# Late attention chunks with the state and the scores stacked on partitions, one product per head

## The chip, the cores and the metric

The kernel runs on one core of one Trainium2 chip. The time is device microseconds (us) of one execution; the figure for a kernel is the median of several runs. In the profile the engines are PE (TensorE matmul), PEld (TensorE weight load), DVE (VectorE), ACT (ScalarE), POOL (GpSimd) and SP (SyncE, which here issues DMAs). SBUF has 128 partitions; PSUM has eight banks of 512 float32 per partition.

## The reference

A linear attention with a decaying state, followed by an MLP with a cosine gate. B = 4 sequences, H = 8 heads, S = 768 steps, D = 48 per head; 3072 tokens of width 384, hidden width 2048.

```python
state = zeros(B, H, D, D)
for t in range(S):
    cur = u * k[t] (outer) v[t]
    y[t] = r[t] @ (state + cur)
    state = w * state + k[t] (outer) v[t]
h = y @ w_in
out = (h * cos(h)) @ w_out
```

`w` and `u` are per head and per element of D. The kernel computes the recurrence in chunks of steps: inside a chunk it needs the masked score matrix A (r times k, each with its share of the decay, above the diagonal; on the diagonal the sum over D of r, u and k, called the bonus here), y = A v + r state, and a new state = w^n (state + k v).

## The kernel before

The MLP takes most of the time. Weights are split in a high and a low part in a float32 format that TensorE runs in one pass, so each product is three matmuls: `mm_h` (L351, 9 matmuls of 384 columns for a block of three 128-token chunks and one 128-wide slice f of the hidden width) and `mm_o` (L357, 9 matmuls). One such step (n, f) has 18 of these. There are 8 blocks of 3 chunks and 16 slices; between `mm_h` and `mm_o` the gate runs over ACT and DVE (L362, L365, L368, L1273, L1276, L1279). Blocks 0 to 3 run interleaved while the weights arrive; blocks 4 to 7 run one after the other.

Attention chunks 0 to 11 (`chunk`) cover the first half of each sequence: one sequence, 128 steps, all 8 heads. Their outputs stay in 12 slots (`R_x`). Chunks 12 to 23 (`late_chunk`) come when slots are free: each covers two sequences (b = 0, 1) of 64 steps and all 8 heads. Before the change the two sequences share the partitions: partitions 0 to 63 hold the 64 steps of b = 0, 64 to 127 those of b = 1 (`half[b]`). Heads go in pairs p = 0 to 3 with parity j = 0, 1; a transposed operand has head j of a pair on partitions 64 j to 64 j + 47, for both sequences.

A late chunk before the change, with its lines:

- loads on SP's queue: pieces of k and r for the transposes (L974), and k, r, v with steps on partitions (L966), all after the score matmuls of the chunk before;
- DVE transposes k and r (L1010); POOL multiplies both with the decay (L1017);
- POOL: r k (L1029), k with its decay (L1035), times u (L1032); DVE sums to the bonus a (L1044);
- ACT writes the diagonals, one instruction per pair and parity: a times an identity (L1053);
- PE: 16 score matmuls, 48 rows high and 64 columns wide, on the four quarters of its array (L1070), and 16 for k v (L1083; the last two chunks leave these out, as no state is wanted after them);
- DVE copies the scores into A where step order allows (L1102, two instructions); ACT spreads the state into a zero-padded tile, parity by parity (L1112); DVE makes the new state (L1120, L1121);
- PE: the product, `mm_xx`: 24 matmuls of the spread state with r, both parities on 112 rows (L1132), then 32 of v with A, 64 rows, one sequence at a time (L1154), summed in the same PSUM banks. An output is written in strips of 32 of the 384 features; a strip that belongs to both heads of a pair gets one matmul from each;
- ACT and DVE write the result to the slots in the split format (L1171, L1176).

The order on each engine's queue is fixed when the kernel is built. `Plan` holds each piece of work as an `op` with engine, due time, modelled cost, what it waits for and its buffers. `one_pass` schedules greedily by earliest start and then by due time, `latest` turns a schedule into new due times (the latest start that keeps its end), and `order` makes FULL such passes, keeps the one with the earliest end, and then searches at random over the work that starts before HORIZON = 110 us. `port=True` marks work on DVE and POOL that the model keeps from overlapping. A `Buf` takes one tile of a ring, and the plan picks which.

Of the kernel before, what the change touches and what calls it, by code (L numbers as in the profile page):

```python
# [33 lines left out]
XS = 12  # L34
# [6 lines left out]
FULL = 6  # L41
HORIZON = 110.0
PASSES = 250
# [37 lines left out]
class Plan:  # L81
# [101 lines left out]
    def order(self, passes):  # L183
# [100 lines left out]
def kernel(  # L284
# [86 lines left out]
    with ExitStack() as actx:  # L371
# [20 lines left out]
        R_A = ring("A", 4, [P, NP, C], F32)  # L392
# [13 lines left out]
        zt = att.tile([KP, 2, NP, 2 * D], F32, name="zt")  # L406
        R_zt = [Tile(zt[:, n]) for n in range(2)]
        R_zt2 = [Tile(zt, R_zt)]
# [128 lines left out]

        def late_table():
            b_tab2 = Buf(B_ATT)

            def tab_t2():
                pt = b_tab2().rearrange("q (p t) -> q p t", p=NP)
                for p in range(NP):
                    for b in range(2):
                        nc.tensor.matmul(pt[b * CT : (b + 1) * CT, p, :], decT_k[:, p, mid], ident, start=True, stop=True)

            def tab_copy2():
                pt = b_tab2().rearrange("q (p j d) -> q (p j) d", p=NP, j=2)
                nc.scalar.copy(dec_k, pt[:, :, 0:D])
# [3 lines left out]
            return o_c2, op(POOL, 110, 0.6, start_late, [last_A[0]], port=True)  # L553
# [179 lines left out]
        def chunk(i, due, xbuf):  # L733
# [128 lines left out]
            def mm_x():  # L862
                x = xv()
                for g in range(NK * 4):
# [3 lines left out]
                        x[gs, g // 4, :], zb()[:, p, G * s : G * s + G], rT()[0:KP, p, :], start=(g < 4), stop=False,  # L868
# [80 lines left out]
        def late_chunk(i, due, xbuf):  # L949
            if not o_dk2:  # L950
                o_dk2.extend(late_table())
            o_late = o_dk2[1]
            m, n_ = (i - XS) % NM, (i - XS) // NM
            t0 = EC * C + n_ * CT
            kb, vb, mb, ab, rb = Buf(R_k), Buf(R_v), Buf(R_f), Buf(R_a), Buf(R_f)
# [4 lines left out]
            half = [slice(b * CT, (b + 1) * CT) for b in range(2)]  # L960
            more = i < NJ - NM

            def load(dst, src):
                def go():
                    for b in range(2):
                        nc.sync.dma_start(  # L966
                            dst()[half[b], :, 0:D], src[2 * m + b, :, t0 : t0 + CT, :].rearrange("h t d -> t h d")
                        )

                return go  # L970
# [31 lines left out]
            l_k = op(SP, due - 5.2, 1.3, load(kb, k), ahead, [kb], lat=2.6, line="late")  # L1002
            l_r = op(SP, due - 5.1, 1.3, load(rn, r), ahead, [rb], lat=2.6, line="late")
            l_v = op(SP, due - 5.0, 1.3, load(vb, v), ahead, [vb], lat=2.6, line="late")
# [9 lines left out]
            def decay_s(dst, dec):  # L1014
                def go():
                    d = late_t(dst)[0:KP]
                    nc.gpsimd.tensor_tensor(  # L1017
                        d, d, dec[0:KP, None, :, mid].to_broadcast([KP, 2, NP, CT]), op=ALU.mult
                    )

                return go

            t_k = op(DVE, due - 2.9, 1.1, tr_s(kT, ks), [l_ks], [ks, kT])
            e_k = op(POOL, due - 2.8, 1.4, decay_s(kT, decT_k), [t_k, o_dtk], [kT], port=True)
            t_r = op(DVE, due - 2.8, 1.1, tr_s(rT, rs), [l_rs], [rs, rT])
            e_r = op(POOL, due - 2.7, 1.4, decay_s(rT, decT_r), [t_r, o_dtr], [rT], port=True)
# [4 lines left out]
            def bonus_u():  # L1031
                nc.gpsimd.tensor_tensor(heads(mb), heads(mb), u_b, op=ALU.mult)  # L1032

            def decay_k():
# [4 lines left out]
            o_mu = op(POOL, due - 2.2, 1.05, bonus_u, [o_m, o_u], [mb], port=True)  # L1039
# [3 lines left out]
                0.5,  # L1043
# [5 lines left out]
            def diagonal(j):  # L1049
                def go():  # L1050
                    for p in range(NP):
                        h = 2 * p + j
                        nc.scalar.activation(A[j]()[:, p, 0:CT], ident2, AF.Copy, scale=ab()[:, h : h + 1])  # L1053
# [3 lines left out]
            o_d = [op(ACT, due - 1.55 + 0.01 * j, 1.1, diagonal(j), [o_a, o_late], [ab, A[j]], line="diagonal") for j in range(2)]  # L1057

            def score(j):
                return sp()[:, j, 0 : NP * CT].rearrange("q (p t) -> q p t", p=NP)  # L1060

            def z_of():
                return sp()[:, :, NP * CT : NP * (CT + D)].rearrange("q b (p e) -> q b p e", p=NP)

            def mm_az():
                for p in range(NP):
                    for j in range(2):
                        ps = slice(j * DP, j * DP + D)
                        for b in range(2):
                            nc.tensor.matmul(  # L1070
                                score(j)[half[b], p, :],
                                late_t(kT)[ps, b, p, :],
                                late_t(rT)[ps, b, p, :],
                                start=True,
                                stop=True,
                            )
                if not more:
                    return
                z = z_of()
                for p in range(NP):  # L1080
                    for j in range(2):
                        for b in range(2):
                            nc.tensor.matmul(  # L1083
                                z[j * DP : j * DP + DP, b, p, :],
                                kb()[half[b], 2 * p + j, :],
                                vb()[half[b], 2 * p + j, 0:D],
                                start=True,
                                stop=True,
                            )
# [4 lines left out]
                1.3 if more else 0.75,  # L1094
                mm_az,
                [e_k, e_r] + ([o_kd, l_v] if more else []),
                [kT, rT, sp] + ([kb, vb] if more else []),
# [3 lines left out]
            def mask(j):  # L1101
                return lambda: nc.vector.copy_predicated(  # L1102
                    A[j]()[:, :, 0:CT], upper2[:, None, :].to_broadcast([P, NP, CT]), score(j)
                )
# [3 lines left out]
            before = [last_z[2 * m], last_z[2 * m + 1], last_z2.get(m)]  # L1108

            def spread(j):  # L1110
                ps = slice(j * DP, j * DP + D)
                return lambda: nc.scalar.copy(zb()[ps, :, :, j * D : (j + 1) * D], zc[m][ps])  # L1112

            o_zt = [op(ACT, due - 1.9, 0.5, spread(j), before, [zb]) for j in range(2)]

            if more:

                def state():
                    w_c = pq[0:KP, None, :, 16:17].to_broadcast([KP, 2, NP, D])
                    nc.vector.tensor_tensor(zc[m], z_of()[0:KP], zc[m], op=ALU.add)  # L1120
                    nc.vector.tensor_tensor(zc[m], zc[m], w_c, op=ALU.mult)  # L1121

                last_z2[m] = op(DVE, due - 1.2, 1.2, state, [o_A, *o_zt, *before, o_pow], [sp])

            def mm_xx():
                x = xp()[:, :, 0 : NK * CT].rearrange("q b (kk t) -> q b kk t", kk=NK)
                for kk in range(NK):
                    for b in range(2):
                        for g in range(4 * kk, 4 * kk + 4):
                            p, s = divmod(g, 3)  # L1130
                            gs = slice(G * (g % 4), G * (g % 4) + G)
                            nc.tensor.matmul(  # L1132
                                x[gs, b, kk, :],
                                zb()[:, b, p, G * s : G * s + G],
                                late_t(rT)[0:KP, b, p, :],
                                start=(kk == 0),
                                stop=False,
                                skip_group_check=True,
                            )

# [6 lines left out]
                for group in rounds:  # L1147
                    for b in range(2):
                        for g, n in group:
                            p, s = divmod(g, 3)  # L1150
                            gs = slice(G * (g % 4), G * (g % 4) + G)
                            parts = {0: ((0, 0),), 1: ((0, G), (1, D)), 2: ((1, DP + 16),)}[s]
                            j, at = parts[n]
                            nc.tensor.matmul(  # L1154
                                x[gs, b, g // 4, :],
                                vb().rearrange("q h d -> q (h d)")[half[b], p * 2 * DP + at : p * 2 * DP + at + G],
                                A[j]()[half[b], p, 0:CT],
                                start=False,
# [4 lines left out]
            xo = op(PE, due - 0.7, 1.8, mm_xx, [e_r, l_v, *e_A, *o_zt], [rT, xp, vb, zb, *A], lat=0.3)  # L1163

            def xv():
                return xp()[:, :, 0 : NK * CT].rearrange("q b (kk t) -> q kk b t", kk=NK)
# [4 lines left out]
            x_h = op(ACT, due - 0.4, 0.47, lambda: nc.scalar.copy(xo_(0), xv()), [xo], [xp, xbuf])  # L1171
# [327 lines left out]
```

## Time and profile before

| | |
|---|---|
| median of 3 runs | 510.2 us (509.86 to 510.3) |
| the profiled execution | 509.76 us |
| its span, first to last instruction | 508.0 us |
| PE busy | 496.5 us, 98% of the span |
| DVE, ACT, POOL busy | 368.1, 328.4, 173.4 us |
| mean granted TensorE clock | 0.998 |

The span is shorter than the profiled execution by what lies before the first and after the last instruction. In a row of the profile, L351 is a line of the kernel, `out<-in` are tile names without buffer numbers, then partitions x elements. The words behind `<-` at the end name what ended the idle time before these instructions. Matmuls are pipelined, so their lengths overlap: the time that one takes from PE is the distance of the starts.

### The profile page before, as it was taken

To read this page: it belongs to the slowest core of one execution; us is meant where nothing else is said; L and a number is where in the kernel's file an instruction comes from. 1 tells how busy PE (TensorE), PEld (TensorE's weight loads), DVE (VectorE), ACT (ScalarE), POOL (GpSimd) and SP (SyncE) were. 2 spreads that over 40 slices of the span, in tenths; PEclk is the share of its full clock that TensorE was granted. 3 is DMA by queue.
4 is the path that set the end of the run, shared out by engine and by line. 5 is a ranking of instruction groups with operands and counts; after the bars stand their busy time and mean duration, and the time that the engine had idled before them with its cause. 6 is when DMAs were issued, how large, how long until landed. Compare 5 with 4: busy or idle time off the path is not lost.

```text
span 508.0 us, 14010 instructions
## 1 busy us (share of the span) xinstructions
PE 496.5 (98%) x5459; PEld 475.6 (94%) x5459; DVE 368.1 (72%) x775; ACT 328.4 (65%) x835; POOL 173.4 (34%) x186
## 2 busy tenths in 40 slices
PE   7999999999999999999999999999999999999994
PEld 5788889999999999999999999999999999999994
DVE  5898988889888865566676776776767757666552
ACT  3989887777767665546576565675756666654452
POOL 6785722365454342233425134223134042200000
PEclk9999999999999999999999999999999999999999
DMA  8987545587765583243576746546455563410001
GB/s 139 160 167 183 91 142 172 186 163 159 176 134 131 112 150 48 34 103 48 137 141 148 143 130 144 116 140 147 119 140 131 143 160 80 116 25 24 2 1 50
DMA packets 128041, 60.15 MB, mean 118 GB/s; under 512 B 103777, under 2 KB 123874, under 8 KB 127970
## 3 DMA queue, kind: packets, MB, share of 16 engines
q1 hardware_dynamic: 122694, 52.02, 42.5%
q0 software_dynamic: 5184, 7.08, 10.2%
q8 instruction: 44, 0.72, 0.6%
q14 instruction: 27, 0.22, 0.1%
q10 hardware_dynamic: 92, 0.10, 0.1%
HBM read 47.39 MB, written 11.80 MB: 116 GB/s over the span
## 4 chain that ended last, share of the span: by engine, by line
PE 95%; DVE 1%; DMA 1%; POOL 1%; ACT 0%; issue 0%; POOLq 0%; DVEq 0%
PE bank L357 41%; PE bank L351 39%; PE bank L880 2%; PE bank L846 2%; PE bank L1132 2%; PE bank L1154 2%; PE bank L772 2%; PE bank L1070 1%; PE bank L867 1%; DMA k<-in_k_dram 1%; PE bank L1083 1%; PE bank L902 1%; PE bank L1345 1%; POOL f L791 0%; POOL k L799 0%; DVE rT L781 0%
## 5 line engine op out<-in xcount | busy, mean ns | idle before, releaser
L357 PE MATMUL bank<-w_out_hi,gh 128*128 128x384 f32 x384 | 132.2, 344 | 0.0
L357 PE MATMUL bank<-w_out_hi,gl 128*128 128x384 f32 x384 | 129.8, 338 | 0.0
L351 PE MATMUL bank<-xh,w_in_lo 128*128 128x384 f32 x384 | 129.6, 337 | 0.0
L357 PE MATMUL bank<-w_out_lo,gh 128*128 128x384 f32 x384 | 129.4, 337 | 0.0
L351 PE MATMUL bank<-xh,w_in_hi 128*128 128x384 f32 x384 | 129.1, 336 | 0.0
L351 PE MATMUL bank<-xl,w_in_hi 128*128 128x384 f32 x384 | 128.7, 335 | 0.0
L362 ACT ACTIVATE qi<-bank 128x384 int32<-128x384 f32 (+1 forms) x132 | 63.2, 482 | 60.2 <-PE bank L351 60.1
L1273 DVE TENSOR_TENSOR bank<-bank,f 128x384 f32<-128x384 f32 (+1 forms) x132 | 72.8, 551 | 39.0 <-ACT f L368 36.1
L368 ACT ACTIVATE f<-f 128x384 f32<-128x384 f32 (+1 forms) x132 | 67.6, 515 | 43.1 <-DVE f L365 39.2
L365 DVE SCALAR_TENSOR_TENSOR f<-bank,qi 128x384 f32<-128x384 f32 (+1 forms) x132 | 71.1, 541 | 33.1 <-ACT qi L362 32.5
L1279 DVE TENSOR_TENSOR gl<-bank,gh 128x384 fp32r<-128x384 f32 (+1 forms) x132 | 71.1, 540 | 25.9 <-ACT gh L1276 25.5
L1276 ACT CAST gh<-bank 128x384 fp32r<-128x384 f32 (+1 forms) x132 | 61.6, 467 | 36.8 <-DVE bank L1273 35.1
L357 PEld LDWEIGHTS bank<-w_out_hi,gh 128*128 128x128 f32 x384 | 72.0, 187 | 2.5 <-DVE bank L1273 0.2
L351 PEld LDWEIGHTS bank<-xh,w_in_hi 128*128 128x128 f32 x384 | 72.1, 188 | 0.6 <-DVE A L853 0.2
L357 PEld LDWEIGHTS bank<-w_out_hi,gl 128*128 128x128 f32 x384 | 72.1, 188 | 0.3 <-DVE gl L1279 0.2
L351 PEld LDWEIGHTS bank<-xh,w_in_lo 128*128 128x128 f32 x384 | 72.2, 188 | 0.0
L351 PEld LDWEIGHTS bank<-xl,w_in_hi 128*128 128x128 f32 x384 | 72.1, 188 | 0.0
L357 PEld LDWEIGHTS bank<-w_out_lo,gh 128*128 128x128 f32 x384 | 72.0, 187 | 0.0
L695 POOL TENSOR_TENSOR f<-f,raw 128x384 int32<-128x384 int32 x32 | 36.3, 1135 | 62.3 <-DVE f L684 14.2
L1017 POOL TENSOR_TENSOR kT<-kT,decT_k 112x512 f32<-112x512 f32 x12 | 15.9, 1327 | 117.2 <-PE bank L351 63.5
L1329 POOL DMA_DIRECT2D out_dram<-f x36 | 32.0, 996 | 44.6 <-ACT f L1313 30.1
L836 ACT ACTIVATE A<-ident,a 128x128 f32<-128x128 f32 x96 | 29.4, 391 | 1.6 <-DVE a L827 1.5
(113 smaller groups left out, 596.3 us busy)
## 6 DMA issues: line engine op xcount, KB each, us to landing
raw<-in_moe_w_in_dram SPq DMA_DIRECT2D x32, 384.0 KB, 3.5
raw<-in_moe_w_out_dram SPq DMA_DIRECT2D x32, 384.0 KB, 3.4
out_dram<-f POOLq DMA_DIRECT2D x36, 192.0 KB, 4.4
raw<-in_k_dram SPq DMA_DIRECT2D x47, 80.0 KB, 2.6
raw<-in_r_dram SPq DMA_DIRECT2D x47, 80.0 KB, 3.3
k<-in_k_dram SPq DMA_DIRECT2D x12, 192.0 KB, 4.0
r<-in_r_dram SPq DMA_DIRECT2D x12, 192.0 KB, 4.2
v<-in_v_dram SPq DMA_DIRECT2D x12, 192.0 KB, 5.0
```

The costliest lines, as they stand in the source:

```text
L351: nc.tensor.matmul(ph, a, b_, start=(i == 0), stop=(i == len(mm) - 1))
L357: nc.tensor.matmul(acc, a[:, ts], b_[:, f, :], start=(first and i == 0), stop=(last and i == 2))
L362: nc.scalar.activation(qi, ph, AF.Copy, scale=INV_2PI, bias=0.25)
L365: nc.vector.scalar_tensor_tensor(q, ph, INV_2PI, qi, op0=ALU.mult, op1=ALU.subtract)
L368: nc.scalar.activation(q, q, AF.Sin, scale=TWO_PI, bias=0.5 * math.pi)
L695: lambda: nc.gpsimd.tensor_tensor(ai(), ai(), cn(), op=ALU.add),
L836: nc.scalar.activation(A[j]()[:, p, :], ident, AF.Copy, scale=ab()[:, h : h + 1])
L1017: nc.gpsimd.tensor_tensor(d, d, dec[0:KP, None, :, mid].to_broadcast([KP, 2, NP, CT]), op=ALU.mult)
L1273: nc.vector.tensor_tensor(g()[:, cs], ph()[:, cs], q()[:, cs], op=ALU.mult)
L1276: nc.scalar.copy(gh()[:, cs], g()[:, cs])
L1279: nc.vector.tensor_tensor(gl()[:, cs], g()[:, cs], f32(gh())[:, cs], op=ALU.subtract)
L1329: nc.gpsimd.dma_start(to, ob()[rows], accum_op=ALU.add)
```

## The change

In a late chunk, steps of both sequences now sit on the same 64 partitions, and the two halves of the partitions belong to the two parities of the heads: partitions `side[j]` = 64 (1 - j) to 64 (1 - j) + 63 hold the steps of the heads of parity j, for both sequences (8 heads e = (b, p) in the free dimension). The other half holds, on `rows[j]` = 64 j to 64 j + 47, the 48 rows of the state. So one tile `wb` holds in its plane j both v (on `side[j]`) and the state (on `rows[j]`), and one tile `ar` holds in its plane j both A and the decayed r. The product of the two planes contracts over v with A and the state with r at once; rows 48 to 63 of plane 0 are cleared once per buffer.

With this, the 24 state matmuls of `mm_xx` go; its 32 others become 128 rows high for j = 0 and 112 for j = 1. The product's PSUM tile is one bank instead of two. The score and k v matmuls keep their number and alternate. POOL writes the decayed r into `ar` in two instructions, one per parity, and the diagonals in two instructions that ACT did in eight. The masks are over 64 partitions and 512 elements instead of 128 and 256. The state addition becomes two instructions. v's three tiles and r's two become one tile of five with two pairs for late chunks. `u` is rearranged once for the new layout, and the late decay table is made by parity. In the planner FULL goes from 6 to 14, and in the passes the due times of late chunks 13 and later are moved ahead by 0 to 3 us (LEAD).

```diff
-FULL = 6
+FULL = 14
+LEAD = 0.75
...
-                o.due = t
+                o.due = t - (LEAD * (n % 5) if XS < o.group < 100 else 0.0)
...
-        R_r = ring("r", 2, [P, H, DP], F32)
-        R_v = ring("v", 3, [P, H, DP], F32)
+        vr = att.tile([P, 5, H, DP], F32, name="vr")
+        R_v = [Tile(vr[:, n]) for n in range(3)]
+        R_r = [Tile(vr[:, n]) for n in range(3, 5)]
+        R_w = [Tile(vr[:, n : n + 2], (R_v + R_r)[n : n + 2]) for n in (0, 2)]
...
-        R_A = ring("A", 4, [P, NP, C], F32)
+        A_all = att.tile([P, 4, NP, C], F32, name="A")
+        R_A = [Tile(A_all[:, n]) for n in range(4)]
+        R_ar = [Tile(A_all[:, n : n + 2], R_A[n : n + 2]) for n in (0, 2)]
...
+        side = [slice((1 - j) * DP, (2 - j) * DP) for j in range(2)]
+        u_2 = Buf([R_zt[0]])
...
             def tab_t2():
...
-                    for b in range(2):
-                        nc.tensor.matmul(pt[b * CT : (b + 1) * CT, p, :], decT_k[:, p, mid], ident, start=True, stop=True)
+                    for j in range(2):
+                        nc.tensor.matmul(pt[side[j], p, :], decT_k[:, p, mid], ident[:, j * DP : (j + 1) * DP], start=True, stop=True)
...
+            def swap_u():
+                for j in range(2):
+                    nc.gpsimd.tensor_copy(
+                        u_2()[side[j]].rearrange("q p x -> q (p x)").rearrange("q (b p d) -> q b p d", b=2, p=NP),
+                        u_b[side[j], None, j::2, :].to_broadcast([DP, 2, NP, D]),
+                    )
...
-            A = [Buf(R_A) for _ in range(2)]
-            sp, xp, zb = Buf(P_ATT), Buf(P_ATT), Buf(R_zt2)
+            wb, ar = Buf(R_w), Buf(R_ar)
+            sp, xp = Buf(P_ATT), Buf(B_ATT)
+            E = 2 * NP
+            rows = [slice(j * DP, j * DP + D) for j in range(2)]
...
+            def plane(buf, j):
+                return buf()[:, j].rearrange("q a b -> q (a b)").rearrange("q (e x) -> q e x", e=E)
+
+            def clear(buf):
+                if id(buf.tile) not in cleared:
+                    cleared.add(id(buf.tile))
+                    nc.gpsimd.memset(plane(buf, 0)[32:DP], 0.0)
...
+            def decay_r():
+                clear(ar)
+                for j in range(2):
                     nc.gpsimd.tensor_tensor(
+                        by_batch(plane(ar, j))[rows[j]], by_batch(late_t(rT))[rows[j]], late_d(decT_r)[rows[j]], op=ALU.mult
                     )
...
-            e_r = op(POOL, due - 2.7, 1.4, decay_s(rT, decT_r), [t_r, o_dtr], [rT], port=True)
+            e_r = op(POOL, due - 2.7, 2.8, decay_r, [t_r, o_dtr], [rT, ar], port=True)
...
             def diagonal(j):
                 def go():
-                    for p in range(NP):
-                        h = 2 * p + j
-                        nc.scalar.activation(A[j]()[:, p, 0:CT], ident2, AF.Copy, scale=ab()[:, h : h + 1])
+                    to = [DP, E, CT]
+                    nc.gpsimd.tensor_tensor(
+                        plane(ar, j)[side[j]],
+                        ident2[side[j], None, :].to_broadcast(to),
+                        ab()[side[j], :, None].to_broadcast(to),
+                        op=ALU.mult,
+                    )
...
-            o_d = [op(ACT, due - 1.55 + 0.01 * j, 1.1, diagonal(j), [o_a, o_late], [ab, A[j]], line="diagonal") for j in range(2)]
+            o_d = [op(POOL, due - 1.55 + 0.01 * j, 1.35, diagonal(j), [o_a, o_late, e_r], [ab, ar], port=True) for j in range(2)]
...
+                for e in range(E):
+                    mm_a(0, e)
+                    mm_a(1, e)
+                    mm_z(1, e)
+                    mm_z(0, e)
...
-            e_A = [op(DVE, due - 1.4 + 0.01 * j, 0.45, mask(j), [o_A, o_d[j], o_late], [sp, A[j]]) for j in range(2)]
+            e_A = [op(DVE, due - 1.4 + 0.01 * j, 0.65, mask(j), [o_A, o_d[j], o_late], [sp, ar]) for j in range(2)]
...
+            o_gap = op(POOL, due - 2.0, 0.1, lambda: clear(wb), [l_v], [wb], port=True)
...
-                    nc.vector.tensor_tensor(zc[m], z_of()[0:KP], zc[m], op=ALU.add)
+                    for j in range(2):
+                        nc.vector.tensor_tensor(state_of(j), z_of(j)[0:D], state_of(j), op=ALU.add)
                     nc.vector.tensor_tensor(zc[m], zc[m], w_c, op=ALU.mult)
...
             def mm_xx():
-                for kk in range(NK):
-                    for b in range(2):
-                        for g in range(4 * kk, 4 * kk + 4):
...
-                            nc.tensor.matmul(
-                                x[gs, b, kk, :],
-                                zb()[:, b, p, G * s : G * s + G],
-                                late_t(rT)[0:KP, b, p, :],
...
-                for group in rounds:
-                    for b in range(2):
+                deep = [P, KP]
+                for b in range(2):
+                    for n_r, group in enumerate(rounds):
                         for g, n in group:
...
                             nc.tensor.matmul(
                                 x[gs, b, g // 4, :],
-                                vb().rearrange("q h d -> q (h d)")[half[b], p * 2 * DP + at : p * 2 * DP + at + G],
-                                A[j]()[half[b], p, 0:CT],
-                                start=False,
+                                w_all[0 : deep[j], at : at + G],
+                                plane(ar, j)[0 : deep[j], b * NP + p, :],
+                                start=(b == 0 and n_r == 0),
...
-            xo = op(PE, due - 0.7, 1.8, mm_xx, [e_r, l_v, *e_A, *o_zt], [rT, xp, vb, zb, *A], lat=0.3)
+            xo = op(PE, due - 0.7, 1.3, mm_xx, [e_r, l_v, *e_A, *o_zt], [ar, xp, wb], lat=0.3)
```

More of the change, by code (lines that the diff above doesn't have):

```diff
@@ L1042, in late_chunk @@
                 due - 1.6,
-                0.5,
+                0.55,
                 lambda: nc.vector.tensor_reduce(ab(), heads(mb), op=ALU.add, axis=AX.X),
@@ L1065, in mm_az, with z_of @@
+            def z_of(j):
+                return sp()[side[j], 1 - j, 0 : E * D].rearrange("q (e d) -> q e d", e=E)
             def mm_az():
-                for p in range(NP):
-                    for j in range(2):
-                        ps = slice(j * DP, j * DP + D)
-                        for b in range(2):
[L1070 to L1089, printed above, removed]
+                def mm_a(j, e):
+                    nc.tensor.matmul(
+                        score(j)[:, e, :], late_t(kT)[rows[j], e, :], plane(ar, j)[rows[j], e, :], start=True, stop=True
+                    )
@@ L1091, in late_chunk, with mm_z @@
+                def mm_z(j, e):
+                    if more:
+                        nc.tensor.matmul(
+                            z_of(j)[:, e, :], kb()[side[j], e, :], plane(wb, j)[side[j], e, 0:D], start=True, stop=True
+                        )
+                for e in range(E):
[3 more added lines that the diff above has]
+                    mm_z(0, e)
             last_A[0] = o_A = op(
@@ L1102, in mask, with state_of @@
                 return lambda: nc.vector.copy_predicated(
-                    A[j]()[:, :, 0:CT], upper2[:, None, :].to_broadcast([P, NP, CT]), score(j)
+                    plane(ar, j)[side[j]], upper2[side[j], None, :].to_broadcast([DP, E, CT]), score(j)
                 )
-            e_A = [op(DVE, due - 1.4 + 0.01 * j, 0.45, mask(j), [o_A, o_d[j], o_late], [sp, A[j]]) for j in range(2)]
+            e_A = [op(DVE, due - 1.4 + 0.01 * j, 0.65, mask(j), [o_A, o_d[j], o_late], [sp, ar]) for j in range(2)]
             before = [last_z[2 * m], last_z[2 * m + 1], last_z2.get(m)]
+            def state_of(j):
+                return zc[m][rows[j]].rearrange("q b p d -> q (b p) d")
+            o_gap = op(POOL, due - 2.0, 0.1, lambda: clear(wb), [l_v], [wb], port=True)
             def spread(j):
-                ps = slice(j * DP, j * DP + D)
-                return lambda: nc.scalar.copy(zb()[ps, :, :, j * D : (j + 1) * D], zc[m][ps])
-            o_zt = [op(ACT, due - 1.9, 0.5, spread(j), before, [zb]) for j in range(2)]
+                return lambda: nc.scalar.copy(plane(wb, j)[rows[j], :, 0:D], state_of(j))
+            o_zt = [op(ACT, due - 1.9, 0.45, spread(j), [*before, o_gap], [wb]) for j in range(2)]
             if more:
@@ L1119, in state @@
                     w_c = pq[0:KP, None, :, 16:17].to_broadcast([KP, 2, NP, D])
-                    nc.vector.tensor_tensor(zc[m], z_of()[0:KP], zc[m], op=ALU.add)
+                    for j in range(2):
+                        nc.vector.tensor_tensor(state_of(j), z_of(j)[0:D], state_of(j), op=ALU.add)
                     nc.vector.tensor_tensor(zc[m], zc[m], w_c, op=ALU.mult)
-                last_z2[m] = op(DVE, due - 1.2, 1.2, state, [o_A, *o_zt, *before, o_pow], [sp])
+                last_z2[m] = op(DVE, due - 1.2, 1.6, state, [o_A, *o_zt, *before, o_pow], [sp])
             def mm_xx():
-                x = xp()[:, :, 0 : NK * CT].rearrange("q b (kk t) -> q b kk t", kk=NK)
-                for kk in range(NK):
-                    for b in range(2):
-                        for g in range(4 * kk, 4 * kk + 4):
-                            p, s = divmod(g, 3)
-                            gs = slice(G * (g % 4), G * (g % 4) + G)
-                            nc.tensor.matmul(
-                                x[gs, b, kk, :],
-                                zb()[:, b, p, G * s : G * s + G],
-                                late_t(rT)[0:KP, b, p, :],
[L1136 to L1139, printed above, removed]
+                x = xp()[:, 0 : 2 * NK * CT].rearrange("q (b kk t) -> q b kk t", b=2, kk=NK)
+                w_all = wb().rearrange("q n h d -> q (n h d)")
                 rounds = (
```

74 lines of the change are left out of this document (41 added, 33 removed).

## The prediction

> **What bounds the kernel now.** I read the page's busy times first, then the busy time by stretches, then the chain that ended last, and then TensorE's own instructions around one late chunk.
>
> ```profile
> PE 496.5 (98%) x5459; PEld 475.6 (94%) x5459; DVE 368.1 (72%) x775; ACT 328.4 (65%) x835; POOL 173.4 (34%) x186
> PE 95%; DVE 1%; DMA 1%; POOL 1%; ACT 0%; issue 0%; POOLq 0%; DVEq 0%
> ```
> ```profile
> 0.00:10.00 10.00, 7.52 (x48) 5.39 (x50) 5.18 (x19) 2.30 (x4) 5.95 (x20) 1.00 0.84 145
> 10.00:20.00 10.00, 9.11 (x164) 7.50 (x164) 7.71 (x15) 9.01 (x29) 7.48 (x9) 1.00 1.02 148
> 20.00:30.00 10.00, 9.42 (x192) 7.68 (x192) 8.20 (x15) 8.66 (x26) 8.33 (x9) 1.00 0.95 181
> 30.00:40.00 10.00, 9.24 (x230) 8.12 (x221) 9.90 (x21) 9.08 (x28) 6.72 (x8) 1.00 0.84 151
> 211.00:445.00 234.00, 234.00 (x3185) 225.05 (x3184) 163.17 (x347) 144.95 (x384) 71.60 (x69) 1.00 0.55 126
> ```
> After each stretch come its length and the busy time of PE, PEld, DVE, ACT and POOL, then the granted clock. The chain is PE for 95%. The whole late attention lies in 211 to 445 us. There PE has no idle time, DVE is idle for 71 us and POOL for 162 us, and the clock is 1.00. What PE no longer has to do there comes off the end one for one, and what other engines get to do there is free until it makes PE wait. The span is 508.0 us, the profiled execution took 509.76 us, and the median of the runs is 510.2 us, 0.4 above it. I make the sum against 509.76 and add the 0.4 at the end.
>
> **What one late chunk costs PE now.** A chunk comes as two detours between MLP matmuls, first scores with the state update, then the product. PE's instructions in order of time (start, length of the group, x count):
>
> ```profile
> 214.96 0.34 PE L357 MATMUL bank<-w_out_lo,gh 128*128 128x384 f32 x1
> 215.23 0.69 PE L1070 MATMUL bank<-rT,kT 48*64 48x64 f32 x32
> 215.74 0.64 PE L1083 MATMUL bank<-v,k 64*64 64x48 f32 x32
> 216.32 0.44 PE L357 MATMUL bank<-w_out_hi,gh 128*128 128x384 f32 x1
> 216.59 0.34 PE L357 MATMUL bank<-w_out_hi,gl 128*128 128x384 f32 x1
> ...
> 219.20 0.34 PE L357 MATMUL bank<-w_out_hi,gl 128*128 128x384 f32 x1
> 219.38 0.34 PE L357 MATMUL bank<-w_out_lo,gh 128*128 128x384 f32 x1
> 219.65 0.88 PE L1132 MATMUL bank<-rT,zt 112*32 112x64 f32 x48
> 220.45 0.86 PE L1154 MATMUL bank<-A,v 64*32 64x64 f32 x64
> 221.24 0.45 PE L357 MATMUL bank<-w_out_hi,gh 128*128 128x384 f32 x1
> 221.53 0.34 PE L357 MATMUL bank<-w_out_hi,gl 128*128 128x384 f32 x1
> ```
> ```profile
> 418.40 0.34 PE L357 MATMUL bank<-w_out_lo,gh 128*128 128x384 f32 x1
> 418.67 0.69 PE L1070 MATMUL bank<-rT,kT 48*64 48x64 f32 x32
> 419.29 0.44 PE L357 MATMUL bank<-w_out_hi,gh 128*128 128x384 f32 x1
> ```
> Each float32 matmul of the code is two instructions here. I work with starts, since lengths overlap. MLP matmuls follow each other every 0.175 us (219.20 to 219.38, rounded), but 0.27 us pass from the last one to L1070 (214.96 to 215.23) and 0.27 from the first one after a detour to the second (216.32 to 216.59): about 0.10 lost on each side. The 32 score instructions take 215.23 to 215.74 = 0.51 us (15.9 ns each) when the z products follow, and 418.67 to 419.29 = 0.62 when an MLP matmul follows, so leaving costs another 0.11. The z products then take 0.58 - 0.11 = 0.47 us (14.7 ns). The state product L1132 takes 0.80 us for 48 (16.7 ns), the v product L1154 0.79 - 0.11 = 0.68 us for 64 (10.6 ns). The second detour is 221.53 - 219.38 - 2 x 0.175 = 1.80 us, of which 0.31 is entering and leaving.
>
> **The product.** The change removes the 24 state matmuls (48 instructions) and keeps 32 matmuls (64 instructions) of the v kind, now 112 or 128 rows high instead of 64, still 32 columns wide on four column groups in turn and 64 moving columns. No row of before has this form. The nearest is L1132: 112 high, all four row groups used, 32 wide, 64 columns, 16.7 ns. That 0.80 us also holds the passage from 112-row to 64-row tiles; if it costs the 0.10 seen on entering, the pitch is 0.70 / 48 = 14.6 ns. Whether 128 rows cost more than 112 can be seen in the early chunks, at 128 moving columns:
>
> ```profile
> 36.59 0.86 PE L867 MATMUL bank<-rT,zt 112*32 112x128 f32 x24
> 37.27 1.08 PE L880 MATMUL bank<-A,v 128*32 128x128 f32 x32
> 38.14 0.86 PE L867 MATMUL bank<-rT,zt 112*32 112x128 f32 x24
> ```
> L867 takes 0.68 us for 24 (28.3 ns), L880 0.87 for 32 (27.2 ns): height makes no difference. I take 16.0 ns: 64 x 16.0 = 1.02, with 0.31 the detour is 1.33 instead of 1.80, -0.47 us a chunk and -5.6 us for twelve. Bounds: at the 10.6 ns of L1154 it is 0.99, so -9.7 us; at the 27.2 ns of L880, as if the moving length did not matter, 2.05, so +3.0 us.
>
> [...]
>
> **Scores and z.** The same 32 and 32 instructions on the same four 64 x 64 quarters, now alternating a score of each parity and a z of each parity. A turn of four goes at its slowest, a score: 64 x 15.9 = 1.02 against 0.51 + 0.47, +0.04 on ten chunks, +0.4 us; at the z pitch it would be -0.4. In the last two chunks there is no z, and the scores now use only two quarters (row group j, column group 1 - j) where before they used four. I expect twice the pitch, 1.02 for 0.51: +0.5 each, +1.0 us (bounds 0 to +1.0).
>
> **The late table**, once:
>
> ```profile
> 74.76 1.09 PE L545 MATMUL bank<-ident,decT_k 128*64 128x128 f32 x16
> 75.78 0.44 PE L357 MATMUL bank<-w_out_hi,gh 128*128 128x384 f32 x1
> ```
> Now 1.02 - 0.11 = 0.91 us, 57 ns each at 128 columns; at 64 columns half, -0.4 us (bounds 0 to -0.5).
>
> **What moves to other engines.**
>
> ```profile
> L1017 POOL TENSOR_TENSOR rT<-rT,decT_r 112x512 f32<-112x512 f32 x12 | 15.6, 1301 | 9.9 <-DVE rT L1010 9.9
> L1032 POOL TENSOR_TENSOR f<-f,u_b 128x384 f32<-128x384 f32 x12 | 12.3, 1022 | 0.5
> L1053 ACT ACTIVATE A<-ident,a 128x64 f32<-128x64 f32 x96 | 24.8, 338 | 1.6 <-DVE a L1044 1.6
> L1102 DVE COPY_PREDICATED A<-upper,bank 128x256 f32<-128x256 int32 x24 | 9.4, 441 | 2.8 <-PE bank L1070 1.9 <-ACT A L1053 0.9
> L853 DVE COPY_PREDICATED A<-upper,bank 128x512 f32<-128x512 int32 x24 | 17.2, 736 | 2.6 <-ACT A L836 1.7 <-PE bank L846 0.8
> L1120 DVE TENSOR_TENSOR zc<-bank,zc 112x384 f32<-112x384 f32 x10 | 5.5, 555 | 4.9 <-PE bank L1083 4.8
> L1010 DVE STREAM_TRANSPOSE kT<-raw 128x512 f32<-128x512 f32 x12 | 8.4, 703 | 0.0
> ```
> Durations go by elements per partition. The decay of r becomes two instructions of 512 elements (+1.3 us POOL a chunk; half that if POOL also gained from 48 rows), and the diagonals go from eight ACT instructions (8 x 0.338 = 2.7 us) to two on POOL (2 x 1.3 = 2.6 us). POOL gets 3.9 us more a chunk, some 43 us for the eleven chunks that do this work after 211 us: 115 of 234 us busy. ACT loses 2.7 a chunk. DVE gets two masks of 512 for two of 256 (+0.6) and one more state addition (+0.56): 13 us more of its 71 us idle. All this is covered as long as a product's inputs come before PE reaches it. The way from the loads to the product grows by 1.3 + 0.6 = 1.9 us. Its cover is the pitch of the chunks, 215.23 to 418.67 us in ten pitches, 20 us each, of which POOL would use 5.7 + 3.9 = 9.6 (5.7 being two decays of 1.3 and three products of 1.02); without it every us late is a us on PE. Behind a POOL instruction that waits stand the next chunk's decays and the output additions of L1329, whose readers have no date before the end. The two new waits (a state spread behind the clearing of the gap, the bonus behind the swapped u) are met long before. The loads keep their number of DMAs and pieces, but v's ring of three becomes two pairs, each held until the product; with 20 us a chunk the pair two chunks back is free before the load is issued. These edits I cost at nothing.
>
> **Sum.** -5.6 + 0.4 + 1.0 - 0.4 = -4.6 us: 509.76 - 4.6 = 505.2 profiled, 505.6 for the median.
>
> **Rivals.**
> *Slower: the tall product runs at the pitch of the other 128-row rows.* Place: PE, second detour. At 27.2 ns it costs +3.0 us, and the sum becomes +4.0: 514.2. It decides from (1.80 - 0.31 - 1.0/12) / 64 = 22 ns on. For it: L880 has the very form but for the moving length. Against: L1132 keeps all row groups busy and goes at 16.7 ns with 64 columns. Chance 0.05.
> *POOL and DVE turn into PE's wait.* PE's order is written from modelled times. The model now has 0.65 for a mask (row 0.736), 0.66 for a transpose (row 0.703), 1.6 for the state (3 x 0.555 = 1.67): 2 x 0.09 + 2 x 0.04 + 0.07 = 0.33 us a chunk too little. If PE stands at each product for that time, 12 x 0.33 = 4.0 us are given back: 509.6, no change. Against: POOL's modelled 2.8 for the split decay of r is above its rows (2.6), and DVE idles 30% of the time. Chance 0.09.
> *The early part is planned anew.* The due times and the number of full passes change, and with them the start of the random search over the first 110 us. PE is not busy for 2.48 + 0.89 + 0.58 + 0.76 = 4.7 us of the first 40. Half as much again is 2.4 us: 508.0; a gain of half the 3.5 us after the first 1.2 us is 503.9. Nothing says which sign. Chance of a loss above 1.5 us 0.08.
> *The tall product runs at the small tiles' pitch*, 10.6 ns: -8.7 in all, 501.5. Chance 0.04.
>
> **How the numbers follow.** The forecast has the remaining 0.74, by itself 503.5 to 507.5. The range for 8 in 10, 502.3 to 509.0, takes in the early part's rival and a pitch from about 12 to 20 ns, and leaves out the tall pitch, most of the POOL case and the smallest pitch. A measurement can tell about 0.2%, 1.0 us, from no change. Faster: the forecast, the fourth rival and most of the early case, 0.84; same: most of the POOL case and what is left of the early one, 0.09; slower: the tall pitch and the worst of the POOL case, 0.07.
>
> **What would show it.** In the changed profile the second detour has one group of 64 instructions 128 or 112 rows high, from start to next start 1.0 to 1.2 us; the state product's group of 48 is gone. Scores and z together stay near 1.0 us, and near 1.0 in the last two chunks alone. POOL is busy near 220 us, ACT near 304, DVE near 381. PE stays without idle time from 211 us to about 440 us. I am wrong if the group takes 1.4 us or more, if PE is named as waiting for POOL or DVE in the late chunks, or if the first 75 us change by more than 2 us.

## The result and the profile after

The changed kernel takes 504.6 us in the median (503.59 to 505.22, four runs) against 510.17 beside it (509.86 to 510.3): a ratio of 0.989, 95% interval 0.9871 to 0.9908, so 4.7 to 6.6 us less. Forecast was -4.6 us, 505.6. A second set of runs gave 504.45 against 510.61, ratio 0.9873 (0.9859 to 0.9888). The profiled execution took 505.22 us, the slowest of the first four; its span is 503.5 us.

From the page of the changed kernel, busy times and chain; then the late stretch (length, busy time of PE, PEld, DVE, ACT, POOL, and the granted clock):

```profile
PE 490.8 (97%) x4883; PEld 470.8 (94%) x4883; DVE 382.4 (76%) x785; ACT 308.0 (61%) x739; POOL 220.3 (44%) x228
PE 93%; DVE 2%; ACT 1%; DMA 1%; POOL 1%; issue 0%; POOLq 0%; DVEq 0%; ACTq 0%
```
```profile
0.00:10.00 10.00, 8.11 (x48) 5.92 (x50) 5.14 (x19) 2.28 (x4) 5.83 (x20) 1.00 0.82 145
10.00:20.00 10.00, 9.22 (x164) 7.51 (x164) 7.71 (x15) 8.91 (x29) 8.09 (x10) 1.00 0.94 146
20.00:30.00 10.00, 9.67 (x201) 7.95 (x204) 7.66 (x15) 8.21 (x26) 6.93 (x8) 1.00 1.24 180
30.00:40.00 10.00, 8.41 (x201) 7.26 (x194) 9.45 (x19) 7.96 (x24) 8.18 (x7) 1.00 0.86 146
40.00:50.00 10.00, 8.94 (x161) 7.60 (x151) 8.77 (x16) 9.49 (x28) 6.81 (x6) 1.00 0.91 182
211.00:445.00 234.00, 234.00 (x2643) 226.19 (x2642) 180.84 (x367) 129.86 (x303) 112.73 (x104) 1.00 0.56 126
```

In the late stretch PE is still busy without a gap and the clock is 1.00, POOL has gone from 72 to 113 us, DVE from 163 to 181, ACT from 145 to 130. In the first 50 us, PE is not busy for 5.65 us; before it was 4.71 (it was busy for all of 40 to 50 us).

PE's instructions in order of time, around the first late chunk, a last chunk without state update, and the late table (most of the alternating rows left out):

```profile
215.12 0.34 PE L352 MATMUL bank<-xh,w_in_lo 128*128 128x384 f32 x1
215.39 0.27 PE L1113 MATMUL bank<-A,kT 48*64 48x64 f32 x2
215.40 0.31 PE L1119 MATMUL bank<-vr,k 64*64 64x48 f32 x3
...
216.47 0.44 PE L358 MATMUL bank<-w_out_hi,gh 128*128 128x384 f32 x1
216.75 0.34 PE L358 MATMUL bank<-w_out_hi,gl 128*128 128x384 f32 x1
...
220.05 0.34 PE L358 MATMUL bank<-w_out_lo,gh 128*128 128x384 f32 x1
220.32 1.11 PE L1186 MATMUL bank<-A,vr 128*32 128x64 f32 x64
221.35 0.44 PE L358 MATMUL bank<-w_out_hi,gh 128*128 128x384 f32 x1
221.63 0.34 PE L358 MATMUL bank<-w_out_hi,gl 128*128 128x384 f32 x1
```
```profile
412.82 0.34 PE L352 MATMUL bank<-xh,w_in_lo 128*128 128x384 f32 x1
413.09 1.15 PE L1113 MATMUL bank<-A,kT 48*64 48x64 f32 x32
414.16 0.44 PE L358 MATMUL bank<-w_out_hi,gh 128*128 128x384 f32 x1
414.44 0.34 PE L358 MATMUL bank<-w_out_hi,gl 128*128 128x384 f32 x1
```
```profile
75.17 0.69 PE L553 MATMUL bank<-ident,decT_k 128*64 128x64 f32 x16
75.78 0.44 PE L358 MATMUL bank<-w_out_hi,gh 128*128 128x384 f32 x1
```

A detour is, as in the prediction, the distance from the last MLP matmul before it to the second after it, less two ordinary distances of 0.175 us. The second detour is 221.63 - 220.05 - 0.35 = 1.23 us (1.80 before). The first is 216.75 - 215.12 - 0.35 = 1.28, as before. Without z it is also 1.28 (414.44 - 412.82 - 0.35) where it was 0.82. Each of the others came out within 0.01 of these. So the late chunks cost PE 12 x 1.28 + 12 x 1.235 = 30.2 us, against 10 x 1.28 + 2 x 0.82 + 12 x 1.80 = 36.0, and the table 0.41 less (75.17 to 75.78 is 0.61, against 1.02): 6.2 us less in all. PE's last matmul ends 4.8 us earlier in the profiled pair, so 1.4 us of it were given back ahead of 75 us in that execution; by the medians of the two sets (5.6 and 6.2 us) it is 0.7 and 0.1.

### The profile page after: what moved, and what is told of

Read it like the earlier page. It is cut to its first block, busy times and chain, and to the rows that moved or that the text cites. A ratio compares the mean times of both kernels' runs of the same rounds, so it can differ in the third digit from the quotient of the medians.

```text
span 503.5 us, 12831 instructions
## 1 busy us (share of the span) xinstructions
PE 490.8 (97%) x4883; PEld 470.8 (94%) x4883; DVE 382.4 (76%) x785; ACT 308.0 (61%) x739; POOL 220.3 (44%) x228
## 4 chain that ended last, share of the span: by engine, by line
PE 93%; DVE 2%; ACT 1%; DMA 1%; POOL 1%; issue 0%; POOLq 0%; DVEq 0%; ACTq 0%
PE bank L358 41%; PE bank L352 40%; PE bank L1186 2%; PE bank L864 2%; PE bank L1113 1%; PE bank L898 1%; PE bank L790 1%; DMA k<-in_k_dram 1%; PE bank L1119 1%; PE bank L885 1%; ACT A L854 1%; PE bank L920 1%; PE bank L1377 1%; POOL k L817 0%; POOL f L809 0%
## 5 line engine op out<-in xcount | busy, mean ns | idle before, releaser
L713 POOL TENSOR_TENSOR f<-f,raw 128x384 int32<-128x384 int32 x32 | 35.2, 1101 | 58.4 <-DVE f L702 36.7
L1055 POOL TENSOR_TENSOR kT<-kT,decT_k 112x512 f32<-112x512 f32 x12 | 15.9, 1328 | 75.6 <-DVE kT L1040 75.6
L1060 POOL TENSOR_TENSOR A<-rT,decT_r 48x512 f32<-48x512 f32 x24 | 31.1, 1295 | 15.7 <-DVE rT L1040 14.6
```

Of the source, the lines that this page charges most:

```text
L713: lambda: nc.gpsimd.tensor_tensor(ai(), ai(), cn(), op=ALU.add),
L1055: nc.gpsimd.tensor_tensor(d, d, late_d(decT_k)[0:KP], op=ALU.mult)
L1060: nc.gpsimd.tensor_tensor(by_batch(plane(ar, j))[rows[j]], by_batch(late_t(rT))[rows[j]], late_d(decT_r)[rows[j]], op=ALU.mult)
```

## The experiments

**The planner's old numbers in the changed kernel.**

```diff
-FULL = 14
-LEAD = 0.75
+FULL = 6
+LEAD = 0.0
```

> The changed kernel with the planner's old numbers (6 full passes, no lead). Theory: the gain is the shorter second detour in the late chunks, and the planner's new numbers only draw another order for the first 75 us. Then the twelve late chunks still cost PE 30.2 us of detours (36.0 before the change), PE has no wait in 211 to 445 us, and the time is 503 to 506 us, with what differs from the changed kernel all ahead of 75 us. Rival: without the lead PE reaches the late products before their inputs; then PE waits for DVE or POOL in the late chunks and the time is 507 us or more.

505.2 us (504.78 to 505.35) against 510.89, ratio 0.9888 (0.9874 to 0.9903). The late chunks cost PE 30.2 us in detours and no product waited. The gain does not need the planner's new numbers.

**The planner's new numbers in the kernel before.**

```diff
-FULL = 6
+FULL = 14
+LEAD = 0.75
...
-                o.due = t
+                o.due = t - (LEAD * (n % 5) if XS < o.group < 100 else 0.0)
```

> The kernel before the change with the planner's new numbers (14 full passes, lead 0.75). Theory: the late detours stay at 36.0 us in sum and the time within 1.5 us of 510.2, by the draw of the first 75 us alone. Rival: the planner's numbers bring a part of the gain, then 508.5 us or less with late detours of 36.0.

513.8 us (511.21 to 515.94) against 510.89, ratio 1.0053 (1.003 to 1.0075): slower, and outside what both expected. The late stretch and the waits of PE show where:

```profile
211.00:445.00 234.00, 231.53 (x3006) 222.47 (x3006) 162.35 (x340) 145.84 (x383) 72.17 (x69) 1.00 0.56 124
```
```profile
PE bank L358 <- DVE gl L1280: 1.6, 1, 1.6
PE bank L1133 <- DVE A L1103: 0.8, 1, 0.8
```

PE stands idle for 2.5 us in the stretch in which it had no gap, and the late detours come to 37.6 us instead of 36.0. One MLP product waits 1.6 us for the gate's last step on DVE, one late product 0.8 us for its mask. What brought these together in this order was not tried. In the changed kernel the same numbers do no such harm.

**The product twice.**

```diff
-                for b in range(2):
+                for b in (0, 1, 0, 1):
                     for n_r, group in enumerate(rounds):
```

> The changed kernel with the 64 product instructions of each late chunk issued twice (the second pass starts the sums anew). Theory: their pitch is 14.5 ns, so the second detour grows from 1.24 to 2.16 us (64 x 14.5 = 0.93) and the time by 12 x 0.93 = 11.1 us. Rival: a pitch of 16.7 ns as in the state product of before, with part of the first pass hidden under entering: 1.07 a chunk, 12.8 us.

515.59 us against 510.89 for the kernel before beside it. That is 11.0 more than the changed kernel's 504.6, and 10.3 if the kernel before is set equal in both sets (510.89 and 510.17). The row and its neighbours:

```profile
220.28 0.34 PE L358 MATMUL bank<-w_out_lo,gh 128*128 128x384 f32 x1
220.54 2.01 PE L1186 MATMUL bank<-A,vr 128*32 128x64 f32 x128
222.48 0.44 PE L358 MATMUL bank<-w_out_hi,gh 128*128 128x384 f32 x1
222.76 0.34 PE L358 MATMUL bank<-w_out_hi,gl 128*128 128x384 f32 x1
```

The detour is 2.13 us, 0.90 more for 64 more instructions: 14.1 ns each. In sum that is 12 x 0.90 = 10.8 us. In the two profiles PE's last MLP matmul starts 11.1 us later than in the changed kernel, and 10.9 of this come after the first 100 MLP matmuls, at some 80 us. So the time follows PE one for one.

**The state's share alone, in the kernel before: the 32 matmuls of v with A are left out.**

```diff
-                                stop=False,
+                                stop=True,
...
-                for group in rounds:
-                    for b in range(2):
-                        for g, n in group:
...
```

> The kernel before the change with the 32 v matmuls of each late product left out, so that only the state's share of the product is computed in the late chunks. The second detour is then 0.10 + 48 instructions + 0.11 + 0.10. Theory: the 0.80 us seen for the 48 instructions before held 0.10 for the passage from 112-row to 64-row tiles, their own pitch is 14.5 ns: the detour is 1.01 us. Rival: the pitch is 16.7 ns: 1.11 us.

```profile
319.36 0.34 PE L357 MATMUL bank<-w_out_lo,gh 128*128 128x384 f32 x1
319.62 0.88 PE L1132 MATMUL bank<-rT,zt 112*32 112x64 f32 x48
320.43 0.45 PE L357 MATMUL bank<-w_out_hi,gh 128*128 128x384 f32 x1
320.71 0.34 PE L357 MATMUL bank<-w_out_hi,gl 128*128 128x384 f32 x1
```

The detour is 320.71 - 319.36 - 0.35 = 1.00 us, the theory's 1.01. Followed by an MLP matmul, the group takes 0.81 us, of which 0.11 is leaving, if leaving costs here what it cost the scores; followed by the 64-row tiles it took 0.80. So the passage from 112-row to 64-row tiles cost 0.10 us too, and the 48 instructions themselves go at (1.00 - 0.31) / 48 = 14.4 ns. The stacked product has no such passage: its tiles are 128 and 112 rows high throughout, and at 14.5 ns an instruction nothing of this size shows beside the 14.4. The time is 501.31 us, 9.6 less than the kernel before beside it, and PE's detours are 12 x 0.79 = 9.5 us shorter: here too the time follows PE.

**Half the height.**

```diff
-                                w_all[0 : deep[j], at : at + G],
-                                plane(ar, j)[0 : deep[j], b * NP + p, :],
+                                w_all[0:DP, at : at + G],
+                                plane(ar, j)[0:DP, b * NP + p, :],
```

> The changed kernel with each product matmul contracting partitions 0 to 63 only (half of its terms are left out): 64 rows high instead of 128 or 112, all on the lower row groups, 32 wide, 64 columns, the same 64 instructions in the same order. [...] Rival: the height itself costs; then the pitch goes to the 10.6 ns of the old v product and the detour to 0.99 us.

The kernel leaves out half of the product's terms.

```profile
264.60 0.34 PE L358 MATMUL bank<-w_out_lo,gh 128*128 128x384 f32 x1
264.87 1.10 PE L1186 MATMUL bank<-A,vr 64*32 64x64 f32 x64
265.89 0.44 PE L358 MATMUL bank<-w_out_hi,gh 128*128 128x384 f32 x1
266.18 0.34 PE L358 MATMUL bank<-w_out_hi,gl 128*128 128x384 f32 x1
```

The detour is 1.23 us, as with full height, and not the rival's 0.99. What made the old v product quick per instruction (10.6 ns) was not its 64 rows. What is left is that it used both halves of the rows in turn, eight places of the array (two halves of the rows by four strips of 32 columns) instead of four: 10.6 ns on eight, 14.4 and 14.5 on four. It also wrote two PSUM banks in turn where the stacked product writes one, but so did the state product, which went at 14.4 ns; the two banks alone are not the reason. How the places work together is not shown, and whether eight places in one bank would go as fast was not tried.

The median, 507.04 us, is above that of the changed kernel, though the detours are the same: three of the four executions had a mean clock of 0.989 or 0.990 (506.86 to 508.5 us), and the one at 0.998 took 504.1.

**Twice the diagonals on POOL.**

```diff
                     to = [DP, E, CT]
-                    nc.gpsimd.tensor_tensor(
+                    for _ in range(2):
+                        nc.gpsimd.tensor_tensor(
...
```

> The changed kernel with both diagonals of each late chunk computed twice on POOL, the planner's cost left as it was, so the order stays. It puts 2 x 1.04 = 2.1 us more on the way to each late product. Theory: the work on POOL lies under the 18 to 22 us between chunks, PE does not wait and the time changes by less than 1 us. Rival: the cover is used up; then PE waits at each late product by up to 2.1 us, 12 x 2.1 = 25 us at most, and 5 us or more are seen.

508.47 us, 3.9 above the changed kernel: neither less than 1 us of change nor 5 or more. PE's waits, and the longest of them:

```profile
PE bank L1187 <- DVE A L1141: 1.7, 4, 0.7
```
```profile
304.32 0.34 PE L358 MATMUL bank<-w_out_lo,gh 128*128 128x384 f32 x1
304.59 0.30 PE L1187 MATMUL bank<-A,vr 128*32 128x64 f32 x4
305.62 1.09 PE L1187 MATMUL bank<-A,vr 112*32 112x64 f32 x60 [0.72 <-DVE A L1141]
```

Four of the twelve products stand: their detours are 1.43, 2.25, 1.85 and 2.22 us instead of 1.23, 2.8 us in sum. At the worst of them, 2.1 us more on POOL cost 1.0, so 1.1 us of cover was left for POOL's work; at the other eight there was 2.1 us or more. The rest is not the diagonals' doing. In the two profiles PE's last MLP matmul starts 3.6 us later than in the changed kernel, and 0.8 of this arise ahead of the first doubled diagonal at 188.9 us: 0.2 ahead of 80 us, and 0.6 at one MLP matmul at 165.7 us that waits for DVE (L1348). The kernel before beside this run was slower too, by 0.7 us.

How little room there was can also be read from the changed kernel's own profile. This is its sixth late chunk, the second mask on DVE and the product on PE:

```profile
321.02 0.74 DVE L1140 COPY_PREDICATED A<-upper,bank 64x512 f32<-64x512 int32 x1
321.82 1.11 PE L1186 MATMUL bank<-A,vr 128*32 128x64 f32 x64
```

The mask ends 0.06 us before the product begins. That is also the time from the end of DVE's work to PE's restart where PE did wait for DVE, in the kernel before:

```profile
11.64 0.69 DVE L781 TENSOR_TENSOR rT<-bank,decT_r 112x512 f32<-112x512 f32 x1 [0.77 <-PE bank L772]
12.39 1.16 PE L846 MATMUL bank<-rT,kT 48*128 48x128 f32 x16 [0.78 <-DVE rT L781]
```

DVE ends at 11.64 + 0.69 = 12.33 there, and PE goes on at 12.39. So at the sixth late chunk DVE had nothing left to spare. At the tenth chunk the distance is 0.11 us, at six others 0.39 to 0.56, and at the remaining four 1.6 to 3.5.

**Other draws of the early part**, with seeds 1 and 2.

```diff
-        rng = random.Random(9)
+        rng = random.Random(1)
```

> The changed kernel with another seed (1) of the planner's random search over the first 110 us. Theory: the late detours stay at 30.2 us and the first 75 us come out anew, so the time lies within 1.5 us of 504.6 with a difference that is all ahead of 110 us. Rival: the changed late chunks cost the early part about 1 us in any draw; then no seed comes below 504.0.

> The same with seed 2: theory within 1.5 us of 504.6, late detours 30.2 us, the difference ahead of 110 us; rival no seed below 504.0.

508.76 us (506.02 to 511.44) with seed 1, 506.19 (504.62 to 509.09) with seed 2, late detours 30.3 and 30.1 us. Both lie outside the theory's 1.5 us, seed 2 only just. Neither fell below 504.0, so the rival is not refuted by them; but the span of 4.5 and 5.4 us within one kernel was not in the theory. It goes with the mean granted clock: seed 2 gave 504.62 and 505.17 us at 0.997 and 0.996, 507.21 and 509.09 at 0.990 and 0.989; seed 1 had no execution above 0.994, so its time at a full clock is not known. The profiled execution of seed 2 (509.09 us), in steps of two us:

```profile
8.00:10.00 2.00, 0.76 (x5) 0.48 (x5) 2.00 (x4) 1.10 (x2) 1.88 (x2) 1.00 1.42 166
10.00:12.00 2.00, 1.80 (x20) 1.59 (x20) 1.20 (x3) 0.76 (x3) 1.98 (x3) 0.85 1.25 141
12.00:14.00 2.00, 1.22 (x10) 0.90 (x10) 1.64 (x3) 1.68 (x6) 1.92 (x3) 0.50 0.22 38
...
18.00:20.00 2.00, 2.00 (x40) 1.62 (x32) 1.61 (x4) 0.84 (x3) 0.85 (x1) 0.94 0.90 169
```

The clock goes to 0.50 (column after POOL) from about 11.4 to 18.2 us, an estimate from the means of 0.85 in the two us from 10 and 0.94 in those from 18, after a stretch in which PE was busy for only 0.76 of 2 us. But this is the smaller part of what that execution lost. After the same 100 MLP matmuls PE is 1.4 us behind the changed kernel's profile, and at 211 us 4.3. The other 3.0 us arise between 115 and 200 us, where the clock is 1.00, at MLP matmuls that wait for the gate; the theory had put all of the difference ahead of 110 us. This is the first of them:

```profile
117.12 0.44 PE L358 MATMUL bank<-w_out_hi,gh 128*128 128x384 f32 x1 [0.22 <-ACT f L1345]
```

Seed 1's profile shows the same: 1.4 us ahead of 80 us with the same mean clock of 0.989, and 2.3 us at such waits between 120 and 145 us. That the low clock sets these waits off is not shown.

**Slices of one tile.** The kernel before, with v's and r's tiles and A's four as slices, which leaves the order on every queue as it was.

```diff
-        R_r = ring("r", 2, [P, H, DP], F32)
...
-        R_v = ring("v", 3, [P, H, DP], F32)
+        vr = att.tile([P, 5, H, DP], F32, name="vr")
+        R_v = [Tile(vr[:, n]) for n in range(3)]
+        R_r = [Tile(vr[:, n]) for n in range(3, 5)]
...
-        R_A = ring("A", 4, [P, NP, C], F32)
+        A_all = att.tile([P, 4, NP, C], F32, name="A")
+        R_A = [Tile(A_all[:, n]) for n in range(4)]
```

> The kernel before the change with v's and r's tiles as slices of one tile and A's four as slices of another, as the change has them; every queue's order stays. Theory: the early part's loss of 0.6 to 1.4 us in the changed kernel comes from its other order, not from the shared tiles, so this stays within 0.5 us of before. Rival: slices of one tile bring waits that separate tiles don't have; then 0.6 us or more are lost, ahead of 75 us.

510.47 us against 510.61, ratio 0.9997 (0.9988 to 1.0006): no cost that can be seen, and by the interval none above 0.3 us.

**More warm-up matmuls, and the changed kernel beside them.**

```diff
-                    n = int(min(o.gap, 6.0) / 0.2)
+                    n = int(min(o.gap, 6.0) / 0.11)
```

> The changed kernel with the gaps ahead of the first score matmuls filled with warm-up matmuls counted at 0.11 us each instead of 0.2, so nearly twice as many. Theory: in some executions PE's idle time between 7 and 13 us lets the granted clock fall to 0.5 for 6.8 us, which costs 2 to 4 us; with the gaps filled this is rarer, the mean clock is 0.995 or more in nearly all executions and the median is 504 to 505 us with a spread below 2 us. Rival: the gaps after the first scores decide; then the clock still falls as often as in the changed kernel run beside it.

> The changed kernel itself on the same chip as the two others. Theory: 504.6 us where the mean clock is 0.995 or more, 2 to 4 us more where it is 0.989 to 0.994, with the clock at 0.5 somewhere in the first 20 us. Rival: the same kernel shows one time whatever its clock in the first 20 us.

With more warm-up: 506.08 us (505.32 to 508.62, the last at a mean clock of 0.989), ratio 0.9919 (0.9903 to 0.9935). The changed kernel: 503.95, 504.08 and 504.83 at 0.996 to 0.997, and 506.16 at 0.994. Filling more gaps cost 1.6 us and did not keep the clock up in every execution, so the expectation failed: two of the six executions had a mean clock below 0.995, against one of four without. The changed kernel's execution at 506.16 us had its dip elsewhere than expected, past 20 us, after PE had been busy for 2.38 of 4 us:

```profile
30.00:34.00 4.00, 2.38 (x48) 1.72 (x40) 3.96 (x8) 3.76 (x11) 3.09 (x3) 1.00 0.86 155
34.00:38.00 4.00, 4.00 (x62) 3.78 (x62) 2.42 (x5) 3.27 (x10) 3.62 (x4) 0.57 0.69 126
```

In the changed kernel's first profile PE was busy for 2.60 us of the same 4, and the clock stayed at 1.00.

No kernel tried here that does the whole work beat the changed one.

## Why the prediction was right

**The bound.** Right: the late stretch paid PE's saving out one for one, shown by the doubled product (10.8 us of detours, 10.9 us of delay) and by the state's share alone (9.5 and 9.6) as well as by the change.

**The product.** The mechanism was right, the term mis-sized: -0.47 us a chunk forecast, -0.565 measured, -6.8 instead of -5.6 us. The term that was off is the pitch of 16.0 ns, chosen between 16.7 and 14.6. The lower end held: (1.235 - 0.31) / 64 = 14.5 ns. The 16.7 had the passage to 64-row tiles in it, as the run with the state's share alone shows; the prediction named this and gave it only part of the weight.

**Four places and eight.** An instruction on four places in turn took longer than one on eight, at 64 rows too, by the run with half the height: 14.5 against 10.6 ns, a factor of 1.37. The product took 0.93 us without entering and leaving. A turn of four places took 58 ns in the old state product (0.70 / 12) and in the stacked one (0.93 / 16); a turn of eight took 85 (0.68 / 8).

**Scores and z.** +0.4 us forecast for alternating them, nothing measured (1.28 and 1.28). That a turn of four goes at its slowest was the author's estimate and no run shows it: the 64 took 1.28 - 0.31 = 0.97 us, 15.2 ns each, between the 15.9 and 14.7 of before. The last two chunks: +0.5 each forecast, +0.46 measured. There the 32 scores take as long alone as with 32 z products (1.28 both): 30.3 ns each on two of the four quarters, against 15.9 on four before. The table: -0.4 forecast, -0.41 measured.

**What moves to other engines.** The busy times came as forecast: POOL 220.3 (220), DVE 382.4 (381), ACT 308.0 (304). By group:

```profile
L1060 POOL TENSOR_TENSOR A<-rT,decT_r 48x512 f32<-48x512 f32 x24 | 31.1, 1295 | 15.7 <-DVE rT L1040 14.6
L1094 POOL TENSOR_TENSOR A<-ident,a 64x512 f32<-64x512 f32 x24 | 26.1, 1088 | 10.1 <-DVE a L1086 8.9
L1140 DVE COPY_PREDICATED A<-upper,bank 64x512 f32<-64x512 int32 x24 | 17.6, 735 | 0.6
```

Durations go by elements per partition here: 48 rows take 1.30 us on POOL as 112 did, 64 rows 0.735 on DVE as 128 did. The diagonals took 1.09 us instead of the 1.3 put down for them. That all this cost nothing was right, but the reason given for it was wrong. The cover is not the 20 us between chunks: the order on PE's queue is fixed, the product stands where the plan expects its inputs, and at one chunk 1.1 us more of POOL work would have used the cover up. On DVE it was used up at one chunk, and at a second all but 0.05 us. That the masks, whose modelled cost was too small, made PE wait nowhere was in part luck.

**The early part.** The forecast left it at nothing with both signs open. It gave back 0.1 and 0.7 us by the medians and 1.4 in the profiled pair. Shared tiles cost at most 0.3 us, by the run that kept the order. The planner's new numbers are not needed for it, as the old ones gave 505.2. The clock had no part in the profiled pair, as it stood at 1.00 in the first 50 us of both. What is left is the other order, in which PE waits for k's decay on POOL:

```profile
PE bank L790 <- POOL k L817: 2.6, 3, 1.4
```

The same wait in the kernel before:

```profile
PE bank L772 <- POOL k L799: 1.0, 2, 0.6
```

That is 1.6 us more in this pair, but the cause is not shown by it. The same wait is 1.6 us in the run with slices of one tile, which has the order of before, and 1.7 in the changed kernel's second profile. The 101st MLP matmul starts at 80.3, 80.9 and 81.3 us in the three profiles with the order of before (the kernel itself, the state's share alone, slices of one tile). In those with the order of the changed kernel and a clock of 1.00 it starts at 81.5, 81.7 and 81.7 (the kernel itself, the product twice, twice the diagonals), and at 82.7 in the two in which the clock fell (the kernel's second profile, 0.57 from 34 to 38 us; half the height, 0.50 from 12 to 16). So one order differs by 1 us from execution to execution, the profiled pair took the earliest of before, and the cause of the 0.1 to 0.7 us stays open.

So -4.6 forecast was -6.2 in the late part and +0.1 to +0.7 in the early part: two errors of opposite sign, the larger one the product's pitch. That they partly cancel is luck.

## What to carry to other kernels

Where PE is busy throughout, price a merged product by the distance of starts in the nearest row, and take entering (0.10 us here), leaving (0.21) and every passage between tile shapes (0.10) out of that distance first. Two products that add into the same output and differ only in what they contract are worth trying in one pass over the contraction rows if both fit: here 112 instructions at 12.3 ns and a passage became 64 at 14.5. Work moved off the bound engine is free only up to the room the written order leaves it (here 1.1 us of POOL's work at the tightest chunk), which a run with that work doubled measures directly.

## What was not expected of the hardware

The mean granted clock differed between executions of one kernel: 0.989, 0.997, 0.990 and 0.996 in the four of seed 2. In the profiled one, at 0.989, the clock fell in the early part. The longest gap of PE ahead of the drop, apart from the 1.20 us before its first matmul, is this one:

```profile
8.77 0.66 PE L529 MATMUL bank<-ident,decT_k 128*128 128x128 f32 x4 [1.11 <-ACT decT_k L521]
```

The clock then stays at 0.50 for 6.8 us, by the estimate above. Executions of that kernel with a mean clock as low took 2.0 to 4.5 us longer than those at 0.996 and 0.997, though in the profiled one only a part of it was lost in the stretch in which the clock fell. In the changed kernel's execution at 506.16 us the clock was 0.57 on the mean of the 4 us from 34, and the execution took 1.3 to 2.2 us longer than the other three. The gap alone does not decide. In the changed kernel with the planner's old numbers PE is busy for as little of the same two us, and the clock stayed at 1.00:

```profile
8.00:10.00 2.00, 0.77 (x5) 0.49 (x5) 2.00 (x4) 1.09 (x2) 1.95 (x2) 1.00 1.24 170
```

What does decide is not shown here. A gap of 1.11 us in seed 2 and one of 1.3 in the changed kernel's second profile, with shorter ones beside them, were followed by the drop; this one, in the changed kernel's first profile, was not, and the clock stayed at 1.00 from 30 to 38 us:

```profile
32.20 0.65 PE L790 MATMUL bank<-ident,k 128*112 128x128 f32 x4 [1.40 <-POOL k L817]
```
